# Attention's softmax with its divisions on GpSimd and one guard and reciprocal per unit, in a kernel of attention and two MoE layers

## The chip, the cores and the metric

The kernel runs on one core of one Trainium2 chip. The metric is the device time of one execution in microseconds (us); the lower the better. The engines are called TensorE (PE; its weight loads PEld), VectorE (DVE), ScalarE (ACT), GpSimd (POOL) and SyncE (SP, which issues DMAs). Each takes its instructions from a queue of its own, in order, and waits on semaphores for the others.

## The reference, cut to what matters

Everything is in float32: two batches of 8 heads, 576 positions, head size 64; then 1152 tokens of 512 columns through two feed-forward layers.

```python
def _attn_ref(q, k, v):                     # S = 576, factor = 4, Sd = 144
    scale = 1.0 / np.sqrt(D)
    def sm_attn(qq, kk, vv):
        s = scale * np.matmul(qq, kk.transpose(0, 1, 3, 2))
        s = s - np.max(s, axis=-1, keepdims=True)
        a = np.exp(s)
        a = a / (np.sum(a, axis=-1, keepdims=True) + 1e-09)
        return np.matmul(a, vv)
    q_d = q.reshape(B, H, Sd, factor, D).mean(axis=3)      # k_d and v_d alike
    out_up = np.repeat(sm_attn(q_d, k_d, v_d), factor, axis=2)
    mask = np.abs(pos[:, None] - pos[None, :]) < factor
    scores = np.where(mask, scale * np.matmul(q, k.transpose(0, 1, 3, 2)), -1000000000.0)
...
    return out_up + out_local                 # softmax of the masked scores, times v

def _moe_ref(x, w_in, w_out):                 # d_ff = 2048
    h = x @ w_in
    return (h * np.tanh(softplus(h))) @ w_out     # "mish"
# then a second layer: 8 experts, relu(x @ w1) @ w2, weighted by a normalized gate P
```

## The kernel before, in words

**Stages.** Attention makes the tokens x of the first MoE layer. It runs in a start (to about 60 us), which makes the first group of 288 tokens, three tiles of 96, and then in three waves, one for each further group, at about 60 to 110, 110 to 150 and 150 to 200 us. In the waves its steps are laid between the matmuls of the first MoE layer by `pump`, so that TensorE has products to do while softmax runs. The first MoE layer lasts to about 370 us, the second to the end.

**What sets the order.** The program is written in one order, and a list scheduler then places each engine's instructions by modelled times. So an edit in one place can shift the order on every engine, elsewhere too.

**Units.** `prep` transposes a pair of heads of k or q on TensorE into PSUM; ScalarE copies it to SBUF (`kT`, or `qT` scaled by 0.125), and VectorE adds up four neighbouring columns each (`kd`, `qd`, the sums from which the means come). A unit of the means (`gunit`, 72 queries, 4 heads) and a local one (`lunit`, 96 queries, 8 heads, a window of 102 keys) each have three steps: `sc` makes scores in two PSUM banks, one for the even heads and one for the odd, and calls `softmax` for each; `tr` transposes the weights `pg` or `pl` on TensorE; `av` multiplies by v. `piped` puts two other units' steps between a unit's `sc` and its `tr`. At the end of a local unit VectorE adds the means' part (L390), ScalarE makes `xhi` (L391), VectorE the remainder `xlo` (L392); the first product of the next group waits for all three tiles of tokens.

**`softmax` before.** For one bank: the negated maximum (L298), its scaling where the scores aren't scaled yet (L300, `gm`), one exponential per head on ScalarE with its sum in `den` (L302), then guard and factor (L304), reciprocal (L305) and the division of all heads by a broadcast multiplication (L306), all three on VectorE. `gm` and `gd` are maximum and sums of the means' units, `lm` and `ld` of the local ones. With two parities, 12 local and 8 means' units make 40 divisions.

**The first MoE layer's part.** Weights arrive as 64-bit floats in halves of 512 KB (`load_w64`, tile `raw64`, two buffers). `w_raw` turns a half into float32 with one instruction on ScalarE (L180) and three of VectorE (L181, L183, L184), and then issues the next load. `split` makes `hi` (ScalarE) and `lo` (GpSimd, L191). `mish` runs between a first product (`gemm1`) and its second (`gemm2`): GpSimd limits `me` (L484), VectorE makes `mm` (L485) and L487 and L489, ScalarE `ghi` (L490), and GpSimd `glo` (L491, while attention runs). `prep_v` adds up v's rows on GpSimd.

## Time and profile before

| | |
|---|---|
| median of 3 runs | 1148.27 us (1145.73 to 1153.63) |
| profiled execution, and the span in its trace | 1140.76 us, 1139.0 us |
| mean granted TensorE clock | 0.975 of full speed |
| busy: TensorE, VectorE, ScalarE, GpSimd | 1086.5, 650.7, 525.8, 416.4 us |

The trace is of the profiled execution alone; a time of the trace is in us from the start of its span. Busy times of engines overlap. A matmul's end is modelled, so TensorE's busy share is not its share of peak.

### The profile page before, as it was taken

What the parts mean: (1) busy time and instruction counts of PE and PEld (TensorE: products, weight loads), DVE (VectorE), ACT (ScalarE), POOL (GpSimd) and SP (SyncE); (2) the same over time, 40 slices, a digit from 0 to 9 for tenths busy, and PEclk for the clock granted to TensorE, in tenths of its full rate; (3) what the DMA queues carried; (4) which work ended last, traced back from release to release, by engine and by line L of the source; (5) the groups of instructions that cost most, each with busy time, mean ns of one, the idle gap of its engine ahead of it and who ended that gap; (6) DMA issues with size and microseconds to landing.
All of it is one profiled execution on the core that took longest, in us unless ns stands there. A gap on an engine that the chain in (4) does not pass through costs nothing.

```text
span 1139.0 us, 19058 instructions
## 1 busy us (share of the span) xinstructions
PE 1086.5 (95%) x7202; PEld 989.8 (87%) x7202; DVE 650.7 (57%) x1423; ACT 525.8 (46%) x1465; POOL 416.4 (37%) x452
## 2 busy tenths in 40 slices
PE   8688999889998899999999999999999999999998
PEld 7576888889998887889988998889998899889996
DVE  6769767796778764463544435445454444544442
ACT  4667677666666634244342443424424244242430
POOL 3342622652734714462240532505315043150400
PEclk9787899999999899999999999999999999999999
DMA  8284510230100210120111201112011021110102
GB/s 183 80 193 135 137 23 2 75 111 1 57 1 20 75 37 20 56 75 19 57 38 37 75 19 56 38 37 74 20 56 42 33 75 31 44 55 21 37 1 83
DMA packets 60199, 63.51 MB, mean 56 GB/s; under 512 B 24204, under 2 KB 44620, under 8 KB 60108
## 3 DMA queue, kind: packets, MB, share of 16 engines
q1 hardware_dynamic: 60108, 62.30, 18.7%
q8 instruction: 56, 0.92, 0.3%
q14 instruction: 35, 0.29, 0.1%
HBM read 59.93 MB, written 2.36 MB: 55 GB/s over the span
## 4 chain that ended last, share of the span: by engine, by line
PE 86%; DVE 6%; DMA 3%; ACT 2%; POOL 2%; issue 1%; SPq 0%; DVEq 0%; ACTq 0%; POOLq 0%
PE w L815 35%; PE acc L776 27%; PE w L503 8%; PE acc L526 7%; PE w L776 4%; PE w L366 1%; DMA raw<-in_q_dram 1%; DMA raw<-in_moe_w_in_dram 1%; ACT pl L302 1%; DVE mm L485 1%; PE acc L442 1%; DVE raw L184 1%; DVE raw L183 1%; PE w L267 0%; PE w L377 0%
## 5 line engine op out<-in xcount | busy, mean ns | idle before, releaser
L815 PE MATMUL w<-wc,hhi 128*128 128x512 f32 x1152 | 362.3, 392 | 0.0
L815 PEld LDWEIGHTS w<-wc,hhi 128*128 128x128 f32 x1152 | 213.5, 188 | 41.9
L815 PE MATMUL w<-wc,hlo 128*128 128x512 f32 x576 | 225.7, 392 | 0.0
L688 POOL TENSOR_TENSOR wc<-raw,wc 128x512 fp32r<-128x512 f32 x64 | 82.1, 1305 | 371.7 <-ACT wc L687 371.4
L776 PE MATMUL acc<-thi,wb 128*128 128x288 f32 x768 | 169.7, 297 | 3.4 <-ACT p L763 3.4
L826 DVE SCALAR_TENSOR_TENSOR yacc<-w,P,yacc 128x512 f32<-128x512 f32 x126 | 94.4, 749 | 131.6 <-PE w L815 131.5
L776 PE MATMUL acc<-xhi,wb 128*128 128x288 f32 x768 | 165.0, 296 | 2.8 <-DVE xlo L554 2.5
L776 PEld LDWEIGHTS acc<-thi,wb 128*128 128x128 f32 x768 | 129.2, 189 | 5.7 <-ACT p L763 3.9
L776 PEld LDWEIGHTS acc<-xhi,wb 128*128 128x128 f32 x768 | 127.3, 188 | 4.7 <-DVE xlo L554 2.7
L815 PEld LDWEIGHTS w<-wc,hlo 128*128 128x128 f32 x576 | 108.1, 188 | 24.1
L763 ACT ACTIVATE p<-acc 128x288 f32<-128x288 f32 x128 | 52.2, 410 | 164.4 <-PE acc L776 161.0
L767 ACT ACTIVATE hhi<-acc 128x288 fp32r<-128x288 f32 x128 | 52.5, 412 | 140.5 <-PE acc L776 118.0
L776 PE MATMUL acc<-tlo,wb 128*128 128x288 f32 x384 | 113.7, 296 | 0.0
L776 PE MATMUL acc<-xlo,wb 128*128 128x288 f32 x384 | 113.7, 296 | 0.0
L676 POOL TENSOR_TENSOR wb<-sums,wb 128x256 fp32r<-128x256 f32 x128 | 97.1, 780 | 14.9 <-ACT wb L675 12.9
L676 POOL TENSOR_TENSOR wb<-raw,wb 128x256 fp32r<-128x256 f32 x96 | 72.5, 758 | 76.0 <-PE acc L776 42.4
L484 POOL TENSOR_SCALAR me<-me 128x288 f32<-128x288 f32 x64 | 64.1, 1001 | 92.8 <-ACT me L483 91.1
L768 DVE SCALAR_TENSOR_TENSOR hlo<-acc,hhi 128x288 fp32r<-128x288 f32 x128 | 57.8, 453 | 61.4 <-ACT hhi L767 61.2
L503 PE MATMUL w<-xhi,hi 128*128 128x288 f32 x256 | 81.4, 319 | 8.5 <-ACT xhi L391 5.4
L794 DVE TENSOR_TENSOR w<-w,p 128x288 f32<-128x288 f32 x64 | 29.5, 461 | 91.6 <-PE w L776 46.0
L503 PE MATMUL w<-xlo,hi 128*128 128x288 f32 x256 | 79.8, 312 | 1.2 <-DVE xlo L392 1.1
L503 PE MATMUL w<-xhi,lo 128*128 128x288 f32 x256 | 78.8, 308 | 0.0
(193 smaller groups left out, 2184.3 us busy)
## 6 DMA issues: line engine op xcount, KB each, us to landing
raw<-in_moe_w_dram SPq DMA_DIRECT2D x64, 512.0 KB
raw<-in_moe_w_in_dram SPq DMA_DIRECT2D x16, 512.0 KB
raw<-in_moe_w_out_dram SPq DMA_DIRECT2D x16, 512.0 KB
vw<-in_v_dram SPq DMA_DIRECT2D x12, 192.0 KB
raw<-in_v_dram SPq DMA_DIRECT2D x8, 288.0 KB
raw<-in_q_dram SPq DMA_DIRECT2D x12, 144.0 KB
out_dram<-yacc SPq DMA_DIRECT2D x6, 256.0 KB
raw<-in_k_dram SPq DMA_DIRECT2D x2, 576.0 KB
```

Source lines behind the costliest of these rows:

```text
L484: POOL.tensor_scalar(out=e, in0=e, scalar1=EXP20, scalar2=None, op0=ALU.min)
L503: PE.matmul(out=bk, lhsT=a[:, kk, o], rhs=b[:, kk, c0:c0 + n], start=(i == 0), stop=(i == 3 * KD - 1))
L526: PE.matmul(out=bk, lhsT=a[:, h, o], rhs=b, start=(first and i == 0), stop=(end and i == 2))
L676: POOL.tensor_tensor(out=t[:, 1], in0=src[u][w], in1=f32(t[:, 0]), op=ALU.subtract)
L688: POOL.tensor_tensor(out=t[:, 1], in0=r[:, a], in1=f32(t[:, 0]), op=ALU.subtract)
L763: ACT.activation(out=t, in_=bk[u, b], func=AF.Copy)
L767: ACT.activation(out=hi, in_=y, func=AF.Relu)
L768: DVE.scalar_tensor_tensor(out=lo, in0=y, scalar=0.0, in1=f32(hi), op0=ALU.max, op1=ALU.subtract)
L776: PE.matmul(out=bk[u, b], lhsT=wb[2 * h + u, w][:, wz, kk, :], rhs=ops[xz][:, k + kk, o + c:o + c + NP], start=(m in (0, 1, 5) and i == 0) ...
L794: DVE.tensor_tensor(out=bk[u, "D"], in0=bk[u, "D"], in1=kept[u, "p1"], op=ALU.add)
L815: PE.matmul(out=bk, lhsT=a[:, f, 128 * j:128 * j + 128], rhs=w[:, b, :], start=(i == 0), stop=(i == 3 * FH - 1))
L826: DVE.scalar_tensor_tensor(out=y, in0=bk, scalar=p, in1=y, op0=ALU.mult, op1=ALU.add)
```

## The change

`softmax` takes the scores and weights of both parities at once. It makes maxima and exponentials for the even heads, then for the odd ones, with the sums in one tile `den` of [rows, 2, heads] (two buffers instead of four); then one guard and one reciprocal for both, and two divisions. These run on GpSimd, except for the odd heads' while the start is being written (`state["start"]`), which stay on VectorE: 5 of the 40. The scaling of the maxima (L300) is gone: `kT` is copied with the scale 1/128 and `qT` with 16, whose product is the 0.125 of before, `kd` sums `kT` in SBUF instead of the unscaled PSUM, and so the means' scores need no scale of their own.

```diff
--- before.py
+++ after.py
@@ -278,8 +278,9 @@
                 qd[b, half] = new(at, [128, HP, SH], F32, "qd", 1)
             dst, ddst = qT[b, half][:, hp, :], qd[b, half][:, hp, :]
         ACT.activation(out=dst.rearrange("p (s r) -> p s r", r=4), in_=view, func=AF.Copy,
-                       scale=1.0 if what == "k" else 0.125)
-        DVE.tensor_reduce(out=ddst, in_=view, axis=AX.X, op=ALU.add)
+                       scale=1.0 / 128.0 if what == "k" else 16.0)
+        DVE.tensor_reduce(out=ddst, in_=dst.rearrange("p (s r) -> p s r", r=4) if what == "k" else view, axis=AX.X,
+                          op=ALU.add)
 
     def prep_v(b, half):
 
@@ -291,19 +292,21 @@
             POOL.tensor_tensor(out=a, in0=a, in1=z[:, :, 2, :], op=ALU.add)
             POOL.tensor_tensor(out=a, in0=a, in1=z[:, :, 3, :], op=ALU.add)
 
-    def softmax(s3, p, scale, rows, tag):
-
-        n, nh, nk = s3.shape
-        nm, den = new(at, [n, nh], F32, tag + "m", 4), new(at, [n, nh], F32, tag + "d", 4)
-        DVE.tensor_reduce(out=nm, in_=s3, axis=AX.X, op=ALU.max, negate=True)
-        if scale != 1.0:
-            DVE.tensor_scalar(out=nm, in0=nm, scalar1=scale, scalar2=None, op0=ALU.mult)
-        for i in range(nh):
-            exps.append(ACT.activation(out=p[:, i], in_=s3[:, i], func=AF.Exp, bias=nm[:, i:i + 1], scale=scale,
-                                       accum_out=den[:, i:i + 1]))
+    def softmax(s3, p, rows, tag):
+
+        n, nh, nk = s3[0].shape
+        den = new(at, [n, 2, nh], F32, tag + "d", 2)
+        for par in range(2):
+            nm = new(at, [n, nh], F32, tag + "m", 4)
+            DVE.tensor_reduce(out=nm, in_=s3[par], axis=AX.X, op=ALU.max, negate=True)
+            for i in range(nh):
+                exps.append(ACT.activation(out=p[par][:, i], in_=s3[par][:, i], func=AF.Exp, bias=nm[:, i:i + 1],
+                                           scale=1.0, accum_out=den[:, par, i:i + 1]))
         DVE.tensor_scalar(out=den, in0=den, scalar1=1e-9, scalar2=rows, op0=ALU.add, op1=ALU.mult)
         DVE.reciprocal(out=den, in_=den)
-        DVE.tensor_tensor(out=p, in0=p, in1=den.unsqueeze(2).to_broadcast([n, nh, nk]), op=ALU.mult)
+        for par in range(2):
+            (DVE if par and state["start"] else POOL).tensor_tensor(
+                out=p[par], in0=p[par], in1=den[:, par].unsqueeze(2).to_broadcast([n, nh, nk]), op=ALU.mult)
 
     def gunit(b, half, q4):
 
@@ -318,10 +321,10 @@
                     o = slice(64 * par, 64 * par + 64)
                     PE.matmul(out=bk[:SH, SD * i:SD * i + SD], lhsT=qd[b, half][o, hp, :], rhs=kd[b][o, hp, :],
                               start=True, stop=True)
-            for par, bk in enumerate(bks):
+            for par in range(2):
                 u[par] = pg[state["pg"] % PB]
                 state["pg"] += 1
-                softmax(bk[:SH, 0:2 * SD].rearrange("p (a b) -> p a b", b=SD), u[par], 1.0 / 128.0, 4.0, "g")
+            softmax([bk[:SH, 0:2 * SD].rearrange("p (a b) -> p a b", b=SD) for bk in bks], u, 4.0, "g")
 
         def tr():
             u["pt"] = new(at, [W, 8 * TQ], F32, "pt", 2)[:SH, 0:8 * SH].rearrange("p (a b) -> p a b", a=8)
@@ -367,7 +370,7 @@
                               rhs=kT[b][o, hp, lo:hi], start=False, stop=(hp == HP - 1))
             for par in range(2):
                 u[par] = pl[(2 * t + par) % PB]
-                softmax(s3[par], u[par], 1.0, 1.0, "l")
+            softmax(s3, u, 1.0, "l")
 
         def tr():
             u["pt"] = new(at, [W, 8 * TQ], F32, "pt", 2)
```

The changed file's line numbers are 1 to 3 above those of before: L298 becomes L301, L304 and L305 one more each, L306 L308; from L390 on it is three more (L393, L395, L487, L488, L490, L492, L494).

**VectorE, end of the first wave, before.** `raw64` is a half of weights, `rawx` and `raw` its float32 form; `w`, `odT` are a local unit's output and the means' part; `me`, `mm`, `ml` are mish's.

```order
L181 TENSOR_SCALAR rawx_1871<-rawx_1871 128x512
L390 TENSOR_TENSOR w_1344<-w_1344,odT_1232 128x384
L183 SCALAR_TENSOR_TENSOR rawx_1871<-raw64_1081,rawx_1871 128x512
L184 SCALAR_TENSOR_TENSOR rawx_1871<-raw64_1081,rawx_1871 128x512
L392 TENSOR_TENSOR xlo_106<-w_1344,xhi_105 128x4x96
L390 TENSOR_TENSOR w_1381<-w_1381,odT_1232 128x384
L485 SCALAR_TENSOR_TENSOR mm_1415<-me_1414 128x288
L390 TENSOR_TENSOR w_1398<-w_1398,odT_1232 128x384
L487 TENSOR_TENSOR me_1414<-mm_1415,w_1377 128x288
L392 TENSOR_TENSOR xlo_106<-w_1381,xhi_105 128x4x96
L181 TENSOR_SCALAR raw_2094<-raw_2094 128x512
L392 TENSOR_TENSOR xlo_106<-w_1398,xhi_105 128x4x96
```

The three additions (L390) stand behind the first step of the half in `rawx` and around its other two; the third remainder (L392) stands behind L181 of the next half.

**VectorE at the same place, after.**

```order
L183 SCALAR_TENSOR_TENSOR raw_2037<-raw64_1572,raw_2037 128x512
L184 SCALAR_TENSOR_TENSOR raw_2037<-raw64_1572,raw_2037 128x512
L488 SCALAR_TENSOR_TENSOR mm_1377<-me_1376 128x288
L393 TENSOR_TENSOR w_1343<-w_1343,odT_1197 128x384
L490 TENSOR_TENSOR me_1376<-mm_1377,w_1339 128x288
L181 TENSOR_SCALAR raw_2037<-raw_2037 128x512
L393 TENSOR_TENSOR w_1360<-w_1360,odT_1197 128x384
L395 TENSOR_TENSOR xlo_106<-w_1343,xhi_105 128x4x96
L183 SCALAR_TENSOR_TENSOR raw_2037<-raw64_1647,raw_2037 128x512
L492 TENSOR_TENSOR me_1376<-me_1376,ml_1378 128x288
L181 TENSOR_SCALAR raw_2183<-raw_2183 128x512
L395 TENSOR_TENSOR xlo_106<-w_1360,xhi_105 128x4x96
```

The second addition printed (L393) is the wave's third. It now stands behind a whole half more (`raw64_1572`) and behind L181 of the half that follows (`raw64_1647`); the last remainder (L395) stands behind L181 of yet another.

**GpSimd, second wave, before.** `vd` are v's sums, `me` and `glo` mish's.

```order
L291 TENSOR_TENSOR vd_1661<-vd_1661,raw4_1555 72x256 x2
L491 TENSOR_TENSOR glo_1562<-me_1558,ghi_1561 128x288
L484 TENSOR_SCALAR me_1644<-me_1644 128x288
L292 TENSOR_TENSOR vd_1661<-vd_1661,raw4_1555 72x256 x2
L484 TENSOR_SCALAR me_1763<-me_1763 128x288
L491 TENSOR_TENSOR glo_1648<-me_1644,ghi_1647 128x288
L491 TENSOR_TENSOR glo_1767<-me_1763,ghi_1766 128x288
L484 TENSOR_SCALAR me_1947<-me_1947 128x288
L491 TENSOR_TENSOR glo_1951<-me_1947,ghi_1950 128x288
```

Nothing but v's sums and mish's two links stand here.

**GpSimd at the same place, after.** `pg` and `pl` are the weights of a means' and a local unit, `gd` and `ld` the reciprocals.

```order
L487 TENSOR_SCALAR me_1715<-me_1715 128x288
L308 TENSOR_TENSOR pg0_98<-pg0_98,gd_1662 72x288
L308 TENSOR_TENSOR pg1_99<-pg1_99,gd_1662 72x288
L494 TENSOR_TENSOR glo_1610<-me_1606,ghi_1609 128x288
L308 TENSOR_TENSOR pg2_100<-pg2_100,gd_1685 72x288
L308 TENSOR_TENSOR pg3_101<-pg3_101,gd_1685 72x288
L494 TENSOR_TENSOR glo_1719<-me_1715,ghi_1718 128x288
L308 TENSOR_TENSOR pl0_94<-pl0_94,ld_1748 96x408
L308 TENSOR_TENSOR pl1_95<-pl1_95,ld_1748 96x408
L308 TENSOR_TENSOR pl2_96<-pl2_96,ld_1799 96x408
L308 TENSOR_TENSOR pl3_97<-pl3_97,ld_1799 96x408
L487 TENSOR_SCALAR me_1890<-me_1890 128x288
```

Two `pg` divisions now stand ahead of one `glo`, two ahead of the next, and four `pl` divisions in a row ahead of the `me` after it.

## Rows read from the trace of the kernel before

**Rows 1.** The page: busy time by engine.

```profile
PE 1086.5 (95%) x7202; PEld 989.8 (87%) x7202; DVE 650.7 (57%) x1423; ACT 525.8 (46%) x1465; POOL 416.4 (37%) x452
```

**Rows 2.** Busy time (instructions) of the engines by stretch; then clock, DMA share, GB/s.

```profile
30.00:60.00 30.00, 19.47 (x196) 16.42 (x196) 21.17 (x49) 17.93 (x55) 10.25 (x8) 0.73 0.34 101
60.00:110.00 50.00, 40.17 (x327) 35.17 (x327) 41.60 (x99) 34.02 (x120) 18.13 (x16) 0.84 0.67 163
110.00:150.00 40.00, 37.49 (x272) 33.27 (x273) 30.74 (x76) 25.67 (x94) 20.16 (x22) 0.84 0.42 109
150.00:200.00 50.00, 48.35 (x474) 42.95 (x474) 34.13 (x91) 36.73 (x141) 12.39 (x15) 1.00 0.06 14
200.00:260.00 60.00, 51.28 (x355) 49.68 (x354) 51.80 (x98) 39.38 (x94) 34.68 (x29) 0.94 0.28 88
...
340.00:400.00 60.00, 53.70 (x385) 51.89 (x384) 49.32 (x113) 39.82 (x107) 36.66 (x41) 0.94 0.14 45
```

**Rows 3.** VectorE by line, 0 to 260: count, busy us, mean ns, idle before.

```profile
L306 DVE TENSOR_TENSOR pl<-pl,ld 96x408 f32<-96x408 f32 x24 | 15.1, 631 | 0.5
...
L306 DVE TENSOR_TENSOR pg<-pg,gd 72x288 f32<-72x288 f32 x16 | 11.0, 690 | 0.2
...
L304 DVE TENSOR_SCALAR ld<-ld 96x4 f32<-96x4 f32 x24 | 5.7, 236 | 5.7 <-ACT pl L302 5.7
...
L282 DVE TENSOR_REDUCE kd<-w 128x72 f32<-128x288 f32 x12 | 5.4, 449 | 3.2 <-ACT kT L280 3.1
L300 DVE TENSOR_SCALAR gm<-gm 72x2 f32<-72x2 f32 x16 | 4.5, 284 | 0.0
L305 DVE RECIPROCAL ld<-ld 96x4 f32<-96x4 f32 x24 | 4.1, 171 | 0.5
...
L304 DVE TENSOR_SCALAR gd<-gd 72x2 f32<-72x2 f32 x16 | 2.6, 161 | 1.0 <-ACT pg L302 1.0
L305 DVE RECIPROCAL gd<-gd 72x2 f32<-72x2 f32 x16 | 2.4, 156 | 0.2
```

**Rows 4.** GpSimd by line, 0 to 260, the same columns.

```profile
L191 POOL TENSOR_TENSOR lo<-raw,hi 128x512 fp32r<-128x512 f32 x18 | 25.9, 1450 | 33.5 <-ACT hi L190 33.3
L491 POOL TENSOR_TENSOR glo<-me,ghi 128x288 fp32r<-128x288 f32 x18 | 15.3, 848 | 46.1 <-ACT ghi L490 46.1
```

**Rows 5.** Two lines of mish, 0 to 260: min/median/max ns.

```profile
L485 DVE SCALAR_TENSOR_TENSOR mm<-me x34: 442/452/1551, 61.7 to 259.1; 128x288 f32<-128x288 f32 x34
...
L487 DVE TENSOR_TENSOR me<-mm,w x18: 436/444/454, 62.3 to 197.8; 128x288 f32<-128x288 f32 x18
```

**Rows 6.** The chain of waits, 100 to 112: start us, us, what.

```profile
100.37 3.76 DMA raw<-in_moe_w_in_dram
...
106.39 0.69 DVE rawx L184
```

**Rows 7.** VectorE in order of time: start, us; in brackets idle and releaser.

```profile
77.07 1.52 DVE L306 TENSOR_TENSOR pg<-pg,gd 72x288 f32<-72x288 f32 x1
...
89.99 0.57 DVE L306 TENSOR_TENSOR pl<-pl,ld 96x408 f32<-96x408 f32 x1
...
91.19 0.69 DVE L184 SCALAR_TENSOR_TENSOR raw<-raw,raw 128x512 uint32<-128x512 uint32 x1
...
104.86 0.43 DVE L181 TENSOR_SCALAR rawx<-rawx 128x512 uint32<-128x512 uint32 x1 [0.83 <-ACT rawx L180]
...
108.30 0.56 DVE L390 TENSOR_TENSOR w<-w,odT 128x384 f32<-128x384 f32 x1
```

**Rows 8.** TensorE's waits, 60 to 110: total us, times, longest.

```profile
PE w L503 <- ACT xhi L391: 3.1, 1, 3.1
```

**Rows 9.** GpSimd in order of time, second and third wave.

```profile
119.84 1.08 POOL L290 TENSOR_TENSOR vd<-raw 72x256 f32<-72x256 f32 x1 [3.50 <-PE w L267]
...
135.93 0.97 POOL L491 TENSOR_TENSOR glo<-me,ghi 128x288 fp32r<-128x288 f32 x1 [0.19 <-ACT ghi L490]
...
154.68 0.80 POOL L491 TENSOR_TENSOR glo<-me,ghi 128x288 fp32r<-128x288 f32 x1 [5.87 <-ACT ghi L490]
```


## The prediction

> **What bounds the kernel now.** I read first the page's totals: TensorE is busy 1086.5 of 1139.0 us and VectorE 650.7 [rows 1], so over the whole program only the 52.5 us in which TensorE stands idle, and the time it spends at the lower of its two clock levels, can be won. Then the windows by stage [rows 2]: the attention that the change touches runs in the start (to 60 us) and in three waves, which I cut at 60, 110, 150 and 200 us. TensorE idles 10.5 us in 30 to 60, 9.8 in 60 to 110, 2.5 in 110 to 150 and 1.7 in 150 to 200. Its mean granted clock is 0.73, 0.84, 0.84 and 1.00 of 2.4 GHz in these stretches, so part of each of the first three ran at 1.2 GHz. The third wave is full and at full clock: nothing is to be had there. The place to look at is 60 to 110, where VectorE is busy 41.6 of 50 us.
>
> Next I asked for TensorE's waits there [rows 8]. The longest is for `xhi`, the second group's tokens, 3.1 us. The chain of waits [rows 6] and VectorE's own order of time [rows 7] say why `xhi` was late. VectorE sat at the head of its queue on the bit rearrangement of a weight half (L181), which waited 0.83 us for ScalarE's L180, and that for a weight DMA of 3.76 us. The additions that end attention (L390) stand behind it. That is a queue whose head waits for a transfer, which less work on VectorE doesn't shorten by itself.
>
> **The change, part by part.** Off VectorE [rows 3]: of 40 divisions all but the five odd ones of the start move, 21 of width 408 and 14 of width 288: 21 x 0.631 + 14 x 0.690 = 22.9 us. The 16 scalings L300 go: 4.5 us. Twelve guards and reciprocals of the local units go, 12 x (0.236 + 0.171) = 4.9, and eight of the mean units, 8 x (0.161 + 0.156) = 2.5. Together 34.8 us of VectorE's time, nearly all between 17 and 200 us.
>
> Onto GpSimd: 35 two-input instructions. No row shows one that broadcasts an operand there. The nearest are `glo` (288 wide, 848 ns) and the weights' `lo` (512 wide, 1450 ns) [rows 4]. On the line between them a column costs (1450 - 848) / 224 = 2.69 ns, so 408 columns cost 848 + 120 x 2.69 = 1171 ns. I take 21 x 1.17 + 14 x 0.85 = 36.5 us, as the shapes lie between those rows; the ends are 35 x 0.85 = 29.7 and 35 x 1.45 = 50.8. GpSimd was busy 60.9 us from 30 to 200 us [rows 2], so it gets some 60% more to do there, still less than its time.
>
> The sum of four of k's columns now reads `kT` behind ScalarE's copy. VectorE already waited there for that copy (3.1 us of idle time before the `kd` reductions, put down to kT, L280) [rows 3]; the length of 449 ns I leave, since the columns read are the same 288. I take 0, between -0.2 and +0.2 us for a reduction on the path. ScalarE's exponentials and copies keep their number, and the scales ride in instructions that are there anyway: 0.
>
> A guard now waits for the exponentials of both parities, where the even heads' division could run under the odd heads' exponentials. In the waves TensorE has two units' work between a unit's scores and its transposes, which covers it. In the start the third local unit has no such cover: its even division, on GpSimd, is 1.17 - 0.63 = 0.5 us longer and stands behind weight splits. Against that, its odd division no longer queues behind an even one. I take +0.5 us, between -1.0 and +1.5.
>
> **The end of the first wave.** Here the relief must show, and here the order changed against it. The two weight buffers turn round as DMA, L180, L181, L183, L184, next issue: from 100.37 to the end of L184 at 107.08 is 6.7 us [rows 6]. In the queue as changed, the third addition of attention stands behind one more weight half, and behind the first step (L181) of yet another. One buffer was freed at 91.88, the end of an L184 [rows 7], and loaded anew. The load of the half in question comes two full turns of that buffer later, and from a load's start to the end of its L181 it was 105.29 - 100.37 = 4.92 us [rows 6, 7]: 91.88 + 2 x 6.7 + 4.92 = 110.2 us, less x, the time by which VectorE gets earlier through the halves before it. Before, the third addition began at 108.30 [rows 7]. Of x the rows give a bound: from 73 to 92 us the queue loses six divisions (four of `pg`, two of `pl`, the first at 77.07, the last at 89.99 [rows 7]), four L300 and about three guards with reciprocals, 4 x 0.69 + 2 x 0.63 + 4 x 0.28 + 3 x 0.32 = 6.1 us. Some of that only becomes waiting for TensorE's scores, so I take x = 4: 106.2, a gain of 2.1 us. The ends are x = 0, a loss of 1.9, and x = 6, a gain of 3.9. Shorter waits before it, for a divided `pg` say, don't come on top: TensorE arrives earlier and waits longer for `xhi`.
>
> **GpSimd in the second wave.** From 119.84 to 136.90 GpSimd works without a pause through v's sums, `me` and `glo` [rows 9]. In the new order two `pg` divisions stand before the last-but-one `glo` of the burst, 2 x 0.85 = 1.7 us. TensorE itself now has that unit's transposes and the next unit's scores ahead of that `glo`, so I take half, +0.9, between 0 and +1.7. Later two `pl` divisions (2.3 us) stand before a `glo`; before it GpSimd sat idle 5.87 us until 154.68 [rows 9], which covers them: 0, up to +2.3 in each of the two later waves when a division comes late into that gap. On SP each pair of v's loads now stands behind one weight load more, as the weights on VectorE run one half further ahead too; the distance to the end of the first wave stays, so I take 0.
>
> **After 200 us** nothing is edited, but the scheduler's choices shift: at eight places up to 340 us one product of the first MoE's two stages changes places with its neighbour, and where the second MoE begins its first products interleave in another way. TensorE idles 8.7 us from 200 to 260 and 6.3 from 340 to 400 [rows 2], for waits at these joints. Nothing says which order is better; I take 0, and a third of those 15.0 us either way, 5.0.
>
> **Sum** against the profiled execution (1140.76 us, 1.8 of it outside the span): +0.5 - 2.1 + 0.9 = -0.7, so 1140.1. The shown runs' median, 1148.27, lies 7.5 above that execution; I forecast for the median 1147.5. With all terms at their ends: -1.0 - 3.9 - 5.0 = -9.9 and 1.5 + 1.9 + 1.7 + 4.6 + 5.0 = +14.7, that is 1138 to 1163, though all seldom fall on one side.
>
> **The shared port.** VectorE's L485, with both inputs in SBUF, ran 442 to 1551 ns, while L487, of the same size with one input in PSUM, stayed in 436 to 454 ns [rows 5]. So an instruction of the first kind is at times held up, and GpSimd was working at such times; L306 belongs to that kind, its mean of 690 ns for 288 columns [rows 3] being well above L487's median of 444.
>
> The Trainium skill's page "SBUF — State Buffer", section "Who interferes with whom", says that VectorE and GpSimd share one port pair as an exclusive lock, taken by a VectorE instruction with two SBUF inputs and by a GpSimd one, and that the loser waits for the whole instruction. The trace agrees: the stretch appears only in the first kind. By that rule each moved division takes the lock for longer than before, 1.17 us instead of 0.63, which speaks against the change; rival C is what it would then do.
>
> **Rivals.** (A) VectorE's throughput was the cause of all that TensorE lost from 60 to 110 us. For it: 41.6 of 50 us busy. Then the 9.8 us of idle time go and with them the slow clock that followed, (1 - 0.84) x 40.17 = 6.4 us: 1124.6, on the median 1132. Against it: L181's wait for a DMA [rows 6, 7]. It decides if the weight halves get through the queue before TensorE asks for the second group. Chance 0.18.
>
> (B) GpSimd becomes the bound. `me` and `glo` are links between a first product and its second, and the new order puts four `pl` divisions in a row ahead of an `me`: 4 x 1.17 = 4.7 us. If TensorE waits for all of it once in each of three waves, that is 14.1 us: 1154.9, on the median 1162. It decides once the divisions come into that row later than ScalarE has `me` ready; against it stand gaps like the 5.87 us one. Chance 0.14.
>
> (C) The relief of VectorE doesn't come about: the moved divisions hold its two-input instructions up. The `pg` divisions themselves lost 16 x (690 - 444) ns = 3.9 us to such stretches [rows 3, 5], on VectorE; were each moved division to hold up one VectorE instruction in full, 35 would give back up to 36.5 us, more than the 34.8 removed. Then x is 0 and the end of the first wave is 1.9 us later instead of 2.1 earlier: 1151.5 on the median. It decides if L485 and the weights' steps come to run beside divisions most of the time; against it, GpSimd is busy in 18.13 of the 50 us of the first wave [rows 2], and would be in some 30. Chance 0.11.
>
> **How the numbers follow.** The forecast keeps 0.57. A measurement of this kernel can tell a difference from none from about 1%, 11.5 us, on. Faster by more is A and 0.03 of the forecast's spread, 0.21; slower by more is B and 0.02, 0.16; within it the rest of the forecast and C, 0.63. The range must take in A's 1132 and the forecast's upper end short of its last us, and may leave out most of B: 1130 to 1160.
>
> **What the profile will show.** VectorE's total near 616 us and GpSimd's near 453; 408-wide divisions on GpSimd near 1.17 us, 288-wide near 0.85. The third L393 of the first wave near 106 us behind an L181 that waited for ScalarE's L180. If A holds, TensorE's idle time from 60 to 110 us falls below 4 us; if B, its waits are for `ghi` and `glo`, with GpSimd's queue full ahead of them; if C, L485's median rises well above its 452 ns. I am wrong if the start moves by over 2 us, or if the stretch after 200 us changes by more than 5.

## The result, and the profile after

Over 20 runs of each kernel the change made it slower: 1154.88 us (1150.24 to 1163.32) against 1147.71 (1141.58 to 1156.87), a ratio of 1.0063 with a 95% interval of 1.0042 to 1.0085. The forecast was 1147.5, no change that can be told; the time lies in its range, but the direction is wrong, and so is the reason given.

The profiled execution of the changed kernel took 1158.7 us, with a span of 1156.9, which is 17.9 longer than the one shown of before. That is more than the medians differ by, so not all of it is the change. Second traces of both kernels (e13, e14) show further down what comes again.

The page of the changed kernel, busy time by engine, answers to [rows 1]:

```profile
PE 1099.7 (95%) x7202; PEld 1000.0 (86%) x7202; DVE 634.2 (55%) x1332; ACT 526.9 (46%) x1465; POOL 446.5 (39%) x487
```

VectorE is relieved by 16.5 us where 34.8 were worked out, GpSimd has 30.1 more. The windows of the changed kernel, with the stretches of [rows 2]:

```profile
30.00:60.00 30.00, 19.05 (x161) 15.61 (x158) 21.47 (x36) 16.70 (x54) 11.69 (x11) 0.60 0.26 74
60.00:110.00 50.00, 38.90 (x290) 33.40 (x291) 39.50 (x71) 33.21 (x116) 29.62 (x27) 0.81 0.71 168
110.00:150.00 40.00, 32.08 (x236) 28.18 (x236) 24.84 (x55) 22.03 (x70) 21.79 (x26) 0.84 0.47 121
150.00:200.00 50.00, 48.16 (x415) 41.94 (x414) 22.00 (x55) 34.18 (x141) 19.49 (x23) 0.91 0.06 14
...
340.00:400.00 60.00, 54.40 (x392) 52.96 (x390) 48.46 (x107) 36.37 (x95) 28.19 (x30) 0.97 0.11 36
```

The stretches are of time, and the changed kernel is some 5 to 18 us behind in them; still they show less VectorE time in every wave, more GpSimd time, and TensorE neither busier nor faster: 32.08 instead of 37.49 us busy in 110 to 150, and a clock of 0.91 instead of 1.00 in 150 to 200. In this trace the third wave, in which the prediction saw nothing to win, had something to lose.

VectorE by line, to 280 us, in the changed kernel (count, busy us, mean ns, idle before), with lines that answer to [rows 3]:

```profile
L183 DVE SCALAR_TENSOR_TENSOR raw<-raw,raw 128x512 uint32<-128x512 uint32 x24 | 21.5, 896 | 0.3
L184 DVE SCALAR_TENSOR_TENSOR raw<-raw,raw 128x512 uint32<-128x512 uint32 x24 | 21.5, 898 | 0.2
L488 DVE SCALAR_TENSOR_TENSOR mm<-me 128x288 f32<-128x288 f32 x35 | 18.0, 515 | 23.2 <-POOL me L487 23.1
...
L305 DVE TENSOR_SCALAR ld<-ld 96x8 f32<-96x8 f32 x12 | 3.3, 274 | 9.0 <-ACT pl L303 9.0
L305 DVE TENSOR_SCALAR gd<-gd 72x4 f32<-72x4 f32 x8 | 3.2, 400 | 1.7 <-ACT pg L303 1.7
```

GpSimd by line, same stretch and columns:

```profile
L308 POOL TENSOR_TENSOR pl<-pl,ld 96x408 f32<-96x408 f32 x21 | 19.2, 931 | 27.7 <-DVE ld L306 24.6 <-ACT ml L489 2.9
L494 POOL TENSOR_TENSOR glo<-me,ghi 128x288 fp32r<-128x288 f32 x18 | 15.8, 880 | 23.5 <-ACT ghi L493 23.3
L308 POOL TENSOR_TENSOR pg<-pg,gd 72x288 f32<-72x288 f32 x14 | 11.3, 822 | 4.4 <-ACT ml L491 2.2 <-DVE gd L306 0.9 <-DVE ld L305 0.9
```

The line of `mm` in the kernel before, 0 to 260 us:

```profile
L485 DVE SCALAR_TENSOR_TENSOR mm<-me 128x288 f32<-128x288 f32 x34 | 19.6, 575 | 8.2 <-POOL me L484 8.0
```

Two things stand out in the idle times. VectorE sits 23.1 us before `mm` for GpSimd's `me`, where it sat 8.0; and GpSimd sits 24.6 us before `pl` divisions for VectorE's reciprocals, where it had no such wait. Each queue takes its instructions in order, and each now waits at its head for the other. Part of such a wait is only that an engine comes early to work that isn't made yet; how late the links themselves are is summed up further down.

How one such knot looks, in the third wave. GpSimd in order of time, changed kernel:

```profile
189.40 0.80 POOL L494 TENSOR_TENSOR glo<-me,ghi 128x288 fp32r<-128x288 f32 x1 [0.70 <-ACT ghi L493]
191.13 1.69 POOL L308 TENSOR_TENSOR pl<-pl,ld 96x408 f32<-96x408 f32 x2 [0.93 <-DVE ld L306]
192.90 0.93 POOL L487 TENSOR_SCALAR me<-me 128x288 f32<-128x288 f32 x1
200.11 1.69 POOL L308 TENSOR_TENSOR pl<-pl,ld 96x408 f32<-96x408 f32 x2 [6.28 <-DVE ld L306]
201.75 0.80 POOL L494 TENSOR_TENSOR glo<-me,ghi 128x288 fp32r<-128x288 f32 x1
```

and VectorE (start, us; in brackets the idle time before):

```profile
190.65 0.17 DVE L305 TENSOR_SCALAR ld<-ld 96x8 f32<-96x8 f32 x1 [1.63 <-ACT pl L303]
...
193.86 0.46 DVE L488 SCALAR_TENSOR_TENSOR mm<-me 128x288 f32<-128x288 f32 x1 [2.81 <-POOL me L487]
195.32 0.58 DVE L301 TENSOR_REDUCE lm<-w 96x4 f32<-96x408 f32 x1 [1.00 <-PE w L369]
...
196.18 0.57 DVE L301 TENSOR_REDUCE lm<-w 96x4 f32<-96x408 f32 x1
```

ScalarE, which makes `me`:

```profile
191.91 0.41 ACT L486 ACTIVATE me<-w 128x288 f32<-128x288 f32 x1 [0.70 <-PE w L506]
```

GpSimd waits 0.93 us for a reciprocal (`ld`), does two `pl` divisions, then `me`. ScalarE had `me` ready at 192.32 and GpSimd takes it up at 192.90, so 0.6 us of VectorE's wait of 2.81 before `mm` is the divisions' doing; for the rest `me` wasn't there yet. The next pair of divisions waits 6.28 us for its reciprocal, with a `glo` behind it. The maxima of the next unit (L301) stand behind `mm`, but with `mm` done VectorE waits a further 1.00 us for TensorE's scores, so at this place the knot did not hold the maxima up. TensorE has pauses here, and this is what followed (TensorE busy, instructions, granted clock, DMA share, GB/s):

```profile
195.00:200.00 5.00, 3.96 (x46) 0.97 0.01 2
200.00:205.00 5.00, 5.00 (x34) 0.50 0.02 3
205.00:210.00 5.00, 5.00 (x30) 0.51 0.00 0
210.00:215.00 5.00, 5.00 (x71) 1.00 0.00 0
```

From 195 to 200 TensorE was busy 3.96 of 5 us; after it the clock is at 0.50, that is 1.2 GHz, for ten us of full work: some 1.04 us of pauses, and 5 us lost to the clock. That the knot made the pauses isn't shown by these lines.

**Where the 17.9 us lie.** I cut each trace's first 400 us into slices of 1 us and summed TensorE's idle time, and its busy time x (1 - granted clock):

| trace | span | idle, us | lost to the clock, us | first product of the first MoE layer begins |
|---|---|---|---|---|
| before | 1139.0 | 45.3 | 22.3 | 54.38 |
| before, second trace (e14) | 1152.0 | 48.3 | 31.6 | 55.58 |
| changed | 1156.9 | 49.1 | 35.7 | 61.11 |
| changed, second trace (e13) | 1156.1 | 47.5 | 34.6 | 62.69 |

Idle and clock together make 17.2 of the 17.9 us between the first traces. Between two traces of the kernel before they make 12.3 of 13.0: one order of instructions, and mostly the clock. So a difference between two traces is no difference between kernels, until it comes again. The second traces of the two kernels differ by 2.2 us in idle time and clock together, and by idle time alone the kernels don't part (45.3 and 48.3, 49.1 and 47.5): where the loss lies on TensorE, these sums don't tell.

### The profile page after: what moved, and what is told of

Its sections match the earlier page's. It is cut to its first block, busy times and chain, and to the rows that moved or that the text cites. A ratio compares the mean times of both kernels' runs of the same rounds, so it can differ in the third digit from the quotient of the medians.

```text
span 1156.9 us, 19013 instructions
## 1 busy us (share of the span) xinstructions
PE 1099.7 (95%) x7202; PEld 1000.0 (86%) x7202; DVE 634.2 (55%) x1332; ACT 526.9 (46%) x1465; POOL 446.5 (39%) x487
## 4 chain that ended last, share of the span: by engine, by line
PE 82%; DVE 8%; ACT 3%; DMA 3%; POOL 2%; issue 2%; POOLq 0%; DVEq 0%; ACTq 0%; SPq 0%
PE w L818 34%; PE acc L779 26%; PE w L506 6%; PE acc L529 6%; PE w L779 4%; DMA raw<-in_moe_w_in_dram 1%; PE w L369 1%; ACT pl L303 1%; DVE raw L184 1%; DVE mm L488 1%; DVE raw L183 1%; POOL me L487 1%; DVE sums L673 1%; POOL lo L191 1%; DVE raw L181 1%
## 5 line engine op out<-in xcount | busy, mean ns | idle before, releaser
L679 POOL TENSOR_TENSOR wb<-sums,wb 128x256 fp32r<-128x256 f32 x128 | 96.9, 775 | 14.8 <-ACT wb L678 6.8
L487 POOL TENSOR_SCALAR me<-me 128x288 f32<-128x288 f32 x64 | 64.2, 1003 | 78.0 <-ACT me L486 72.3
```

The source lines that it names most:

```text
L487: POOL.tensor_scalar(out=e, in0=e, scalar1=EXP20, scalar2=None, op0=ALU.min)
L679: POOL.tensor_tensor(out=t[:, 1], in0=src[u][w], in1=f32(t[:, 0]), op=ALU.subtract)
```

## The experiments

All ratios are to the kernel before, run on the same chip: 12 runs of each edited kernel against 35 of before (17 for e15). e1 to e4, e5 to e8, e9 to e12 and e13 to e15 ran on a chip each, so kernels of different groups are compared by their ratios. Line numbers in a run's lines are those of its own kernel, shifted by its edit.

One rival stands beside every experiment: each edit makes the list scheduler place other instructions anew. Of TensorE's first 2800 instructions 94% keep their sequence between the changed kernel and e5, and 93 to 95% between before and e6, e10 or e12 (longest common sequence, by names and shapes). Those three lie within 0.1% of before, so a shift of that size did not by itself move the time; no run holds the order fixed.

### Which half of the program: e1, e2

e1 keeps the start's guards and divisions as before and changes the waves; e2 the reverse. Both scale through k and q as the change does.

```diff
 def softmax(s3, p, rows, tag):
+    if state["start"]:            # e2: if not state["start"]
+        for par in range(2):      # own den, guard and reciprocal for each parity
...
+            DVE.tensor_tensor(out=p[par], in0=p[par], in1=den..., op=ALU.mult)
+        return
```

> In the start every parity has its own guard and reciprocal and all ten divisions run on VectorE, as before the change; the three waves are as changed. Theory S (the loss is made in the start, where a guard that waits for both parities and a division on GpSimd stand on the path to the first product): the first product of the first MoE layer begins near 55 us instead of 61.1, and the ratio to before falls from 1.006 to 1.000 or 1.001. Theory W (the loss is made in the waves, by the weight halves ahead of attention and by GpSimd's lock on VectorE): the first product is early too, but the waves lose it again, and the ratio stays at 1.005 or more.

> The start is as changed (one guard for both parities, even divisions on GpSimd); in the waves every parity has its own guard and reciprocal and all divisions run on VectorE. Theory S: the first product begins near 61 us and the ratio to before is 1.005 or more. Theory W: the waves take back the start's delay in the idle time they have anyway, and the ratio is 1.000 to 1.002.

e1: 1152.66 us, ratio 1.0029 (0.9995 to 1.0063). e2: 1149.55, ratio 1.0002 (0.998 to 1.0023). In e1's trace the first product begins at 56.53, 4.6 us earlier than in the changed kernel's, but the second group's first product at 119.81 instead of 118.18: in this trace the first wave had lost it all. In e2's it begins at 61.79, late as in the changed kernel, and the time is that of before. e1's ratio lies between the two theories' and its interval reaches both; e2 decides, since its interval ends below that of the changed kernel (1.0042 to 1.0085). Theory S, the start, falls: a late start doesn't make a late end. The loss is in the waves.

### Which half of the edit: e3, e4, e12

e3 has the joint guard with all divisions on VectorE; e4 divisions on GpSimd with a guard for each parity; e12 only the scaling through k and q.

```diff
 e3:
-            (DVE if par and state["start"] else POOL).tensor_tensor(
+            DVE.tensor_tensor(
 e4, e12: guard, reciprocal and division inside "for par in range(2)", den [n, nh] with 4 buffers
```

> One guard and reciprocal per unit as changed, but all 40 divisions on VectorE. If the joint guard is what delays the start, the first product begins at 58 us or later and the ratio is 1.003 or more; if the divisions on GpSimd are what costs, the first product begins near 55 us and the ratio is 1.001 or less.

> Divisions on GpSimd as changed (35 of 40), but each parity with its own guard and reciprocal as before. If the joint guard is what delays the start, the first product begins near 56 us and the ratio is 1.002 or less; if the divisions on GpSimd and their hold on VectorE cost it, the ratio is 1.005 or more.

> Of the change only the scaling through k and q: kT copied with 1/128, qT with 16, kd summed from kT, L300 gone; every parity has its own guard, and all divisions run on VectorE. The prediction's terms give 16 x 0.28 = 4.5 us less on VectorE and 0 on the path: 0.997 to 1.001. If the joint guard is what made one guard with all divisions on VectorE faster (0.996), this run is at 0.999 or more; if the scaling did, at 0.997 or less.

e3: 1144.79, ratio 0.9962 (0.994 to 0.9985). e4: 1151.61, ratio 1.0032 (1.0006 to 1.0058). e12: 1147.45, ratio 0.9991 (0.9967 to 1.0016). The joint guard isn't the cost; with the divisions left on VectorE it is faster than before, though e3's first product begins at 60.04. The scaling alone can't be told from nothing. Moving the divisions to GpSimd costs 1.0063 - 0.9962 = 1.0% with the joint guard, and 1.0032 - 0.9991 = 0.4% without it, the latter only just clear of the noise. A late first product marks neither half: it begins at 60.91 in e4 and at 60.21 in e12, which has no joint guard and no division on GpSimd.

### What about a division on GpSimd costs: e5 to e8, e11

e5 takes `me`'s limit off GpSimd while attention runs, e11 `glo` instead; e6 and e7 make e5's edit in the kernel before and in e3. e8 is e3 with 35 idle instructions of the divisions' shape on GpSimd, into a tile that nobody reads.

```diff
 e5, e6, e7:
-        POOL.tensor_scalar(out=e, in0=e, scalar1=EXP20, scalar2=None, op0=ALU.min)
+        (DVE if s < ATT_END else POOL).tensor_scalar(out=e, in0=e, scalar1=EXP20, scalar2=None, op0=ALU.min)
 e11:
-        (POOL if y is e else DVE).tensor_tensor(out=glo, in0=y, in1=f32(ghi), op=ALU.subtract)
+        DVE.tensor_tensor(out=glo, in0=y, in1=f32(ghi), op=ALU.subtract)
 e8, beside e3's edit:
+            if not (par and state["start"]):
+                z = sham[0:n, 0:nh * nk].rearrange("p (a b) -> p a b", b=nk)
+                POOL.tensor_tensor(out=z, in0=z, in1=den[:, par]..., op=ALU.mult)
```

> The changed kernel, but while attention runs (18 of the products' pairs) the limit on me, mish's first link, is taken on VectorE instead of GpSimd. Theory Q (the divisions on GpSimd cost because me stands behind them in GpSimd's queue, and VectorE's queue then waits at mm for me): VectorE's wait for GpSimd's me, 17.8 us in the trace of the changed kernel, is gone, and the ratio to before falls from 1.006 to 1.000 or less, as with all divisions on VectorE (0.996). Theory P (the division is itself later on GpSimd, and TensorE's transposes wait for it; or it holds VectorE's two-input instructions up): nothing of that changes, VectorE has 18 instructions more, and the ratio stays at 1.005 or more.

> The kernel before with the same edit, as the control of the run before this one. Theory Q: VectorE waited 7.7 us for GpSimd's me there too, but without divisions ahead of it; the gain is small, 0.997 to 1.000. If it gains as much as the changed kernel does (0.5% or more), the edit helps whatever the divisions do, and the run before this one tells nothing for Q.

> One guard and reciprocal per unit, all divisions on VectorE, and me's limit on VectorE while attention runs. Both theories: near the ratio of all divisions on VectorE, 0.994 to 0.998; with it the changed kernel with me on VectorE can be compared: Theory Q says that the two differ by less than 0.3%.

> One guard and reciprocal per unit and all 40 divisions on VectorE, as in the run at 0.996, and besides 35 instructions on GpSimd of the divisions' shape and inputs' kind that write a tile nobody reads; they wait for the reciprocals, as the divisions would. Theory Q, and any theory by which GpSimd's time or its hold on VectorE costs: the ratio rises from 0.996 to 1.002 or more. Theory P in its first form (only the transposes' wait for a division on GpSimd costs): it stays at 0.996 to 0.999.

> The changed kernel, but glo, mish's last link, on VectorE instead of GpSimd while attention runs; me stays on GpSimd. If the cost is GpSimd's fullness in general, taking 18 instructions of 0.85 us off it helps like taking me off did (0.997): 0.997 to 1.000. If it is me's place in GpSimd's queue, with VectorE's queue waiting at mm for it, the ratio stays at 1.003 or more.

| kernel | median, us | ratio (95%) |
|---|---|---|
| e5, changed, `me` on VectorE | 1146.09 | 0.9968 (0.9933 to 1.0002) |
| e6, before, `me` on VectorE | 1148.70 | 1.0004 (0.9969 to 1.0039) |
| e7, e3 and `me` on VectorE | 1144.27 | 0.9952 (0.9917 to 0.9987) |
| e8, e3 and idle work on GpSimd | 1159.12 | 1.0097 (1.0063 to 1.0131) |
| e11, changed, `glo` on VectorE | 1153.77 | 1.0032 (1.0006 to 1.0058) |

e5 decides. The 35 divisions are still on GpSimd, TensorE's transposes still wait for them there, and VectorE has 18 instructions more; yet the loss is gone, and e5 stands 0.2% from e7, which has no division on GpSimd. The same edit does nothing for the kernel before (e6). With the divisions on VectorE it hardly matters where `me` runs (e3 0.9962, e7 0.9952); with the divisions on GpSimd it makes 0.95% (1.0063, e5 0.9968). So neither of the two costs by itself on GpSimd; what cost was `me` in one queue with the divisions.

Theory P falls with that. One part of it e5 leaves: with no `me` waiting ahead of them the divisions come sooner too. From a reciprocal's end to the division's end, summed over the 30 of the waves, it takes 45.3 us in e5, 58.8 and 54.6 in the two traces of the changed kernel. But TensorE did not wait longer for them: just before its transposes of `pg` and `pl` it stood idle 5.4 and 5.5 us from 62 to 225 in the changed kernel, 4.8 and 5.6 before, 4.0 in e5.

e5 also weighs the port. VectorE by line, to 280 us, in e5:

```profile
L488 DVE SCALAR_TENSOR_TENSOR mm<-me 128x288 f32<-128x288 f32 x39 | 24.6, 632 | 6.6 <-POOL me L487 6.2
L183 DVE SCALAR_TENSOR_TENSOR raw<-raw,raw 128x512 uint32<-128x512 uint32 x24 | 22.2, 924 | 0.2
L184 DVE SCALAR_TENSOR_TENSOR raw<-raw,raw 128x512 uint32<-128x512 uint32 x24 | 20.0, 837 | 0.1
```

L183's mean is 924 ns and `mm`'s 632, more than in the changed kernel (896, 515), L184's 837 less (898), in a kernel that is as fast as e7. The stretch is real and doesn't reach the end here.

e8 rose as Theory Q had it, by 1.35%, but not for Q alone: its `mm` waited only 1.8 us in all for `me` from 62 to 220. There VectorE's divisions and GpSimd's copies of them start together after the same reciprocal, and VectorE's are held up. VectorE in order of time, e8, then GpSimd:

```profile
83.19 0.16 DVE L308 RECIPROCAL gd<-gd 72x4 f32<-72x4 f32 x1
...
83.62 3.72 DVE L313 TENSOR_TENSOR pg<-pg,gd 72x288 f32<-72x288 f32 x2
```

```profile
83.43 0.78 POOL L312 TENSOR_TENSOR sham<-sham,gd 72x288 f32<-72x288 f32 x1 [0.21 <-DVE gd L308]
84.18 1.25 POOL L193 TENSOR_TENSOR lo<-raw,hi 128x512 fp32r<-128x512 f32 x1
85.40 0.78 POOL L499 TENSOR_TENSOR glo<-me,ghi 128x288 fp32r<-128x288 f32 x1
86.15 0.87 POOL L312 TENSOR_TENSOR sham<-sham,gd 72x288 f32<-72x288 f32 x1
```

Two `pg` divisions, 0.45 us each where nothing disturbs them, took 3.72, while GpSimd ran four instructions without a pause. So e8 shows that work on GpSimd costs even where nobody waits for its result, not by which way. e11 lies between: 15.8 us of `glo` off GpSimd bring 0.3% (an interval that touches the changed kernel's), 18 instructions of `me` 0.95%. It is less how full GpSimd is than what stands behind a waiting head.

A sum over all traces goes with that. For each of the 18 pairs of products that run beside attention I took the time from the end of ScalarE's instruction to the start of the link that it feeds (in the changed kernel L486 and `me`'s limit, L493 and `glo`), less 0.06 us each:

| kernel | `me` late, us | `glo` late, us | ratio |
|---|---|---|---|
| e15 | 4.2 | 4.1 | 0.996 |
| e7 | 6.9 | 7.6 | 0.995 |
| e3 | 8.6 | 5.8 | 0.996 |
| e5 | 2.3 | 9.1 | 0.997 |
| before; second trace | 6.9; 8.6 | 6.9; 6.1 | 1 |
| e6 | 6.3 | 4.3 | 1.000 |
| e2 | 7.5 | 4.5 | 1.000 |
| e12 | 11.4 | 5.8 | 0.999 |
| e10 | 8.8 | 9.6 | 0.999 |
| e8 | 11.6 | 7.3 | 1.010 |
| e1 | 14.1 | 12.4 | 1.003 |
| e4 | 11.4 | 12.2 | 1.003 |
| e11 | 16.0 | 4.7 | 1.003 |
| e9 | 12.5 | 15.0 | 1.004 |
| changed; second trace | 12.8; 13.0 | 15.4; 14.8 | 1.006 |

Where the two links together are 8 to 18 us late, the time is that of before or better; where 21 to 28, slower. e8 stands apart, slowest at 19, for the reason given. The two go together; that the lateness makes the time is what e5 to e7 show, not this table.

### The weights' buffers: e9, e10

Three buffers for weight halves instead of two; to make room a scratch tile of the second layer is cut to what it uses.

```diff
-R64 = 2
+R64 = 3
```

> The changed kernel with three buffers for weight halves instead of two. Theory W (the prediction's reading: the end of the first wave is set by the turn of two weight buffers, DMA, ScalarE, three steps of VectorE, next load): the second group's first product, 118.2 us in the trace of the changed kernel, comes 4 us or more earlier and the ratio to before falls to 1.003 or less. Theory Q (GpSimd's queue with me, divisions and glo makes the loss): the loss of the second and third wave stays, and the ratio is 1.004 or more.

> The control: the kernel before with three buffers for weight halves. Theory W: the second group's first product, 109.95 us in the trace of the kernel before, comes 2 to 4 us earlier, and the ratio is 0.996 to 0.998. If the turn of the buffers doesn't bind, 0.999 to 1.002.

e9: 1154.18, ratio 1.0043 (1.0018 to 1.0068). e10: 1147.11, ratio 0.9994 (0.9965 to 1.0023). TensorE's longest waits from 62 to 125 us, in the changed kernel,

```profile
PE w L506 <- ACT xhi L394: 3.7, 1, 3.7
```

and in e9:

```profile
PE w L506 <- ACT xhi L394: 1.8, 2, 1.4
```

The wait for `xhi` shrinks from 3.7 us at one place to 1.8 at two, and the end gains 0.2%, no more than the intervals leave open. But the second group's first product comes no earlier: at 120.38 in e9 (changed 118.18, in its second trace 125.16), at 115.18 in e10 (before 109.95 and 115.08). In part that is because the layer's first product is itself late there (65.34 and 61.13). So these runs don't say what the turn of the two buffers is worth to the first wave (Theory W); they do say that a third buffer brings before's time down by nothing that can be told, and that with it the change still loses 0.4%.

### Second traces, and the start once more: e13, e14, e15

> The changed kernel once more, for a second trace. If the loss sits where the first trace has it, TensorE's idle time and slow clock to 400 us are again 15 us or more above those of the first trace of the kernel before, VectorE waits 15 us or more for GpSimd's me in the waves, and the clock falls in the third wave. What doesn't come again is chance of one execution.

> The kernel before once more, for a second trace. Its first trace, at 1140.76 us, lies near the lower end of its runs; a second one nearer to the median (1148) should show 5 us or more of added idle time and slow clock to 400 us, and VectorE's wait for GpSimd's me again at 10 us or less.

> The start with a guard for each parity and divisions on VectorE as before; in the waves one guard per unit, divisions and me's limit on VectorE. The first product should come near 55 us instead of 61.6 of the run with me on VectorE and one guard throughout (0.995). If the start's delay reaches the end, the ratio falls to 0.990 to 0.992; if the first wave takes it up, it stays at 0.994 to 0.998.

e13 (one run, 1157.89 us) and e14 (one run, 1153.73) gave the second traces of the table above. e13's idle time and slow clock to 400 us are 14.5 us above those of before's first trace, just short of the 15 expected, and 2.2 above the second. What came again in the changed kernel: the late first product (61.11, 62.69; before 54.38, 55.58) and the two waiting queues. GpSimd's waits from 62 to 220 us in e13, then VectorE's:

```profile
POOL pl L308 <- DVE ld L306: 29.3, 6, 7.9
...
POOL me L487 <- ACT me L486: 14.8, 8, 3.8
```

```profile
DVE mm L488 <- POOL me L487: 18.3, 11, 3.1
```

In the second trace of before VectorE's same wait is

```profile
DVE mm L485 <- POOL me L484: 9.0, 6, 3.0
```

and no wait of GpSimd for a reciprocal exists. What didn't come again is the fall of the clock from 200 to 210 us: in e13 the same two pauses stand at 200.20 and 201.28, TensorE was busy 4.08 of 5 us from 200 to 205, and the clock stayed full until 233; it was down from 86 to 103 instead. The two waiting queues are the change's; when the clock falls differs between executions of one kernel.

How the late links reach the end stays open: TensorE's waits for mish's results, where they should show first, did not grow. From 62 to 220 us, e13:

```profile
PE acc L529 <- ACT ghi L493: 2.3, 3, 1.0
...
PE acc L529 <- POOL glo L494: 1.6, 2, 1.4
```

and e14:

```profile
PE acc L526 <- ACT ghi L490: 3.4, 4, 1.3
```

with 0.6 us for `glo`: 3.9 us in the changed kernel and 4.0 before; in the first traces 3.0 and 7.9.

e15 (the start as before, e7's waves): 1143.67, ratio 0.9959 (0.9924 to 0.9994). TensorE's first product in e15,

```profile
57.54 0.61 PE L517 MATMUL w<-xhi,hi 128*128 128x288 f32 x1 [2.42 <-ACT xhi L405]
```

and in e7:

```profile
61.58 0.61 PE L506 MATMUL w<-xhi,hi 128*128 128x288 f32 x1 [2.05 <-ACT xhi L394]
```

4.0 us earlier; at the second group's first product 1.2 (115.11 and 116.29), in the second wave 0.4, and in the ratio nothing. The first two waves take the start's delay up. e7, e3 and e15 beat before by 0.4 to 0.5%, clear of noise by their intervals; among them nothing can be told.

## Why the prediction was wrong, point by point

- **What bounds it.** Right that TensorE's pauses and the clock before 200 us are all there is to win or lose. Wrong that the third wave is out of play: with nothing to win it was left out of the sum, and in the changed kernel's first trace it lost 5.4 us (the first-stage product that began at 177.20 before came 12.8 us later, that of 193.10 came 18.2 later), most of it to the clock; in the second trace 0.9. So a regular loss there isn't shown either.
- **VectorE's relief, 34.8 us.** It shows as 16.5. Of the edited lines 31 us went (guards and reciprocals took 4.6 off, not 7.4, as a joint `gd` guard took 400 ns in the mean where a single one took 161; one of the eight took 1.22 us), `mm` took 2.9 us less, and L181, L183 and L184 grew by 8.0 us and the second step of `me` (L492) by 2.6. The rest is overlap of neighbouring instructions, which lines count twice and the total once. That the growth comes of more work on GpSimd beside them is likely and was not tried by itself.
- **GpSimd's load, 36.5 us.** 30.5 measured: a 408-wide division took 857 to 1311 ns, mean 931, not 1171; a 288-wide one 822, not 848. The line drawn through two shapes of other instructions was too steep.
- **The shared port.** The prediction read from two lines that only instructions with two SBUF inputs are stretched. That is wrong in the very trace it read: a guard with one input (L304, median 166 ns) took 1.23 us beside a `lo` of GpSimd, and ended when that did. VectorE and GpSimd, before:

```profile
30.38 1.23 DVE L304 TENSOR_SCALAR ld<-ld 96x4 f32<-96x4 f32 x1
```

```profile
30.08 1.50 POOL L191 TENSOR_TENSOR lo<-raw,hi 128x512 fp32r<-128x512 f32 x1
```

- **The sum of k's columns, 0.** Right: 443 ns for `kd` against 449, and e12 is at 0.9991.
- **The start, +0.5.** Mis-sized: +6.7 and +8.3 in two traces. TensorE in the start of the changed kernel:

```profile
25.71 5.25 PE L445 MATMUL acc<-identb 128*128 128x128 bf16 x91
33.60 0.35 PE L336 MATMUL w<-ident,pg 72*72 72x72 f32 x3 [2.64 <-DVE ld L306]
...
55.05 0.85 PE L380 MATMUL w<-ident,pl 96*102 96x96 f32 x4 [4.98 <-DVE pl L308]
...
61.11 0.61 PE L506 MATMUL w<-xhi,hi 128*128 128x288 f32 x1 [2.44 <-ACT xhi L394]
```

By the prediction's own sign (a start that moves by over 2 us) it was wrong here. The lines show the warm-up matmuls (L445) run out 2.64 us before the first transpose and the third local unit wait 4.98 us for its division, and the clock is at 0.50 from 40 us on. What made that isn't shown: before, too, TensorE waited 2.72 us at its first transpose, and the first product is as late in e12 (60.21, no joint guard and no division on GpSimd) and in e10 (61.13, the kernel before with one buffer more). And this term does not reach the end (e2, e15): the step that failed in the sum is not here.
- **The end of the first wave, -2.1.** The mechanism was read rightly. VectorE in order of time, changed kernel:

```profile
115.81 0.43 DVE L181 TENSOR_SCALAR raw<-raw 128x512 uint32<-128x512 uint32 x1 [0.79 <-ACT raw L180]
116.16 0.56 DVE L393 TENSOR_TENSOR w<-w,odT 128x384 f32<-128x384 f32 x1
```

The third addition stands behind an L181 that waited 0.79 us for ScalarE's L180, as forecast, at 116.16 instead of 106.2; before it was at 108.30, and the start's delay is 6.7 of the 7.9 us between. So the gain didn't come; how much was lost, single traces can't say (122.78 in the second trace, 113.21 in before's second). A slip in the sum: with x = 6 the gain would have been 4.1, not 3.9.
- **GpSimd in the later waves, +0.9, and 0 for `pl` before `glo`.** This is the step that failed. The gap of 5.87 us that was to cover the divisions is a gap in time of before; in the queue as changed the divisions don't run in it, they wait in it, for reciprocals that VectorE hasn't made yet. `me` and `glo` behind them wait too, and the sum had no term for `me` at all. In place of +0.9 and 0, GpSimd waited 24.6 us for reciprocals ahead of `pl` divisions, the two links came 28.2 us late in sum, against 13.8, and the median rose by 7.2; e5 takes `me` out of that queue and the loss is gone.
- **Rival B** named the place (`pl` divisions ahead of `me`) and the point from which it decides. Its price, 14.1 us, took TensorE to wait for it in full, and its sign, waits for `ghi` and `glo`, did not come (3.0 and 3.9 us, before 7.9 and 4.0); the medians give 7.2. So it was right on the place and not on the way to the end. Against e3, which has the divisions on VectorE, it is 1.0%, or some 11 us.
- **Rival A**, VectorE's throughput, did not come: TensorE's idle time from 60 to 110 us is 11.1 us, not below 4. e5 and e7 speak against it as well: 35 divisions off VectorE bring nothing there (0.9968 against 0.9952). e3, which lightens VectorE only by guards and L300, gains 0.4%; that it is throughput isn't shown.
- **Rival C**, the port. The Trainium skill's page "SBUF — State Buffer", section "Who interferes with whom", says that a VectorE instruction with two SBUF inputs contends with a GpSimd instruction that reads SBUF. The rows agree on the stretch (L183 from 796 to 896 ns, L184 from 781 to 898). C's sign, a risen median of `mm`, did not come (457 ns; 458 before in the same stretch), and e5 shows that the stretch of L183 can stand without the time's moving.
- **After 200 us.** The last product of the first layer and the end are 16.9 and 17.9 us later in the first traces, against 18.2 in the third wave: within the 5 us given.

What stays open: whether the joint guard makes it cheaper on VectorE (0.3%) and dearer on GpSimd (0.3%), neither of which is clear of the noise, and by which way the late links reach the end. A possible reason for the first, four divisions in a row behind two reciprocals, was argued from the order and not tried by itself.

## What to carry to other kernels

Before moving work to an engine with time to spare, look at what stands behind it in that engine's queue, and at what it will wait for there: an instruction that waits at the head of an in-order queue delays every link behind it, and an idle gap in the old trace says nothing about that. Here moving the short link off that queue too (e5), or leaving the divisions where they were (e3), took the loss away. And before reading a difference of two traces as the change's, take each trace twice.

## What the runs showed of the hardware

- The clock can make most of the spread between executions. Two traces of the kernel before differ by 13.0 us in span, of which 9.3 are TensorE's work at the lower clock and 3.0 its idle time. In the changed kernel's first trace pauses of about 1 us in a stretch of 5 were followed by ten us at half clock; in its second trace the same pauses were followed by full clock.
- A broadcast division of 96 x 408 on GpSimd took 0.86 us at the least, `lo` of 128 x 512 1.26 (before): 0.68 of the time for 0.80 of the width.
- GpSimd's work holds VectorE's up, with one input as with two: a guard of 0.17 us took 1.23 beside a `lo` and ended with it, and two divisions of 0.45 us took 3.72 while GpSimd ran four instructions in a row (e8).
